# A recurrent attention kernel: working tiles allocated in the prepass, three buffers for the last tokens' V, seven late weight units, and other places for two stores in the loop

## The chip, the cores and the metric

The kernel runs on one core of one Trainium2 chip. The metric is the device time of one execution in microseconds (us). The time before is the median of three runs, 1682.81 us (1679.15 to 1693.0).

The core has five engines with a queue of instructions each: PE (matrix products), ACT and DVE (copies and elementwise work), POOL (a few elementwise operations and transfers), and SP, which only issues transfers. Engines wait for each other by semaphores. In the profile PE's weight loads have a row of their own, PEld.

## The reference

Two attention branches over the same 2048 tokens of 640 features, mixed by a gate. Branch A is recurrent: 64 segments of 32 tokens, each with 8 memory tokens ahead of it; the memory of a segment is the output of the segment before.

```python
for s in range(n_seg):                       # 64, seg_len 32, M = 8 memory tokens
    xs = x[:, s * seg_len:(s + 1) * seg_len, :]
    h = jnp.concatenate([mem, xs], axis=1)   # 40 tokens
    q, k, v = (jnp.einsum('btd,dhe->bhte', h, W) for W in (Wq, Wk, Wv))   # 32 heads of 192
    scores = jnp.einsum('bhqe,bhke->bhqk', q, k) * scale
    p = _softmax(jnp.where(mask, scores, -1e9), axis=-1)
    o = jnp.einsum('bhte,hed->btd', jnp.einsum('bhqk,bhke->bhqe', p, v), Wo)
    mem = o[:, :M, :]
    outs.append(o[:, M:, :])
...
g = sigmoid((x * gate_w).sum(-1))
return g * A(x) + (1 - g) * B(x)             # B: dilated local attention, not recurrent
```

## The kernel before

The program runs in four stretches.

**Part B** (`part_b`) computes branch B for all tokens, leaves the result and the gate in `bsc_dram`, and writes the tokens of all segments, transposed, to `xh_dram`. Behind it the first weights of branch A are loaded.

**The prepass** (`prepass`) projects the last 8 tokens of each of the 64 segments ahead of the loop, since they don't depend on the memory. First Q and K, by tiles `ZS` of two buffers that ACT's queue stores to `zpk_dram`; then V: three column groups `t` by four token groups `st`, 20 matmuls each (L548) into four PSUM banks, copied by ACT and DVE in turn (`evac`, L73 and L75) into a tile `ZV` of two buffers, and stored to `zpk_dram` by four transfers on ACT's queue (L555). PSUM holds eight banks, so two such steps. Before the V steps `load_late(1)` (L429) loads 24 weight units into the space that Q and K have left; it issues on SP.

**Part A** (`part_a`) is the recurrence. Its working tiles are allocated at its start: `PP` (aP: queries and values of a segment), `KW` (aK: keys, probabilities, output), `vz` (aVz), `sel` (aSel: selectors and masks that `build_sel` makes with DVE memsets and POOL's affine selects, reading ones from aP), `h_` (aH: the 40 tokens, transposed) and `a4` (aG). Weights don't all fit: 21 half units, listed in `STREAM`, are loaded again in each segment through seven slots (`wst`). `pump` issues such a load on SP as soon as the slot is free, that is when PE has used the unit that was there (`release`); `held` stops the issue, `stage` lets it go on. All engines' orders are written out by hand (`manual_schedule`).

A segment has two parts. The **head** projects the queries and keys of the first two thirds: `m_qk(i, kcs)` are the matmuls (L714; i even for queries, odd for keys), `c_qk(i)` ACT's copy out of PSUM (L721) and `t_qk(i)` DVE's transposition (L731, L734). The copy of i = 2 goes by way of `KW[:, 512:1024]`, all others by aP. The head also finishes the segment before: `pick` copies the new memory into aH, `tail` and `mix` (L664) blend the output, and `store_z` (L648, on POOL) writes the outputs of the 8 tokens from two places, `zst = [KW[:, 640:832], vz[:, 0:192]]`, to `oz_dram`. The **rest** does i = 4 and 5, the values (`m_v`, L811, `c_v`, L819), scores, softmax, the products with the values (`pv_half`, copied out by `c_o`, L853, and `c_z`, L859) and the output projection (`o_group`, L874: columns "oa" and "ob").

The loop (L1017) runs over segments 1 to 62: rest of one, head of the next, 62 passes. It resets its semaphores in a staggered way: the body has four stages (`tc.stage_boundary`), and no engine enters a stage before all engines have said that their work of the stage but one before is done. `done(engine)` in the code is where an engine waits for its own work of the previous stage, its transfers too, and says so. In the head the stage begins with `stage()`, followed by the stores and `done(POOL)`; `done(SP)` and `done(PE)` stand at its end.

**Part Z** (`part_z`) multiplies the outputs of the 512 tokens of the prepass with the output weights and writes them.

Of the kernel before, what the change touches and what calls it, by code (L numbers as in the profile page):

```python
# [10 lines left out]
BF = mybir.dt.bfloat16  # L11
# [2 lines left out]

SLOTS = 7
N_EARLY = 9
LATE0 = 101376
STREAM = [("q", 0, 1, 1), ("k", 0, 1, 1), ("k", 0, 3, 1), ("q", 1, 1, 0), ("k", 1, 0, 0), ("k", 1, 3, 1), ("q", 2, 2,
          0), ("k", 2, 0, 1), ("k", 2, 1, 1), ("k", 2, 4, 1), ("v", 0, 3, 1), ("v", 1, 1, 0), ("v", 1, 4, 1), ("v", 2,
# [7 lines left out]
class _K:  # L27
# [381 lines left out]
    def weights_setup(self):  # L409
        nc, tc = self.nc, self.tc  # L410
        rest = [k for u in self.slice_keys() for k in self.parts(u) if k not in STREAM]
        first = ["q", "k", "v", "oa", "ob"]
        rest = sorted(rest, key=lambda k: first.index(k[0]))
        self.early, late = rest[:N_EARLY], rest[N_EARLY:]
        self.late = ([], [], late[-3:])
        used = 0
        for k in late[:-3]:
# [85 lines left out]
    def prepass(self):  # L503

        nc, tc, KC = self.nc, self.tc, self.KC
# [3 lines left out]
        with tc.tile_pool(name="pre_zv", bufs=2, side="right", reuse_waits="tile") as zvp:  # L509
            zTi = zvp.tile([128, KC, NZ], BF, name="zTi", bufs=1)  # L510
            with tc.tile_pool(name="pre_zs", bufs=2, reuse_waits="tile") as zp, \
                    tc.tile_pool(name="pre_zt", bufs=1, reuse_waits="tile") as ztp:
                zT = ztp.tile([128, KC, NZ], BF, name="zT")
                nc.scalar.dma_start(zT[:], self.zT_dram[:].rearrange("p c s i -> p c (s i)"))
                nc.gpsimd.tensor_copy(zTi[:].rearrange("p c (i s) -> p c i s", i=8),
                                      zT[:].rearrange("p c (s i) -> p c i s", i=8))
                for m in ("q", "k"):
                    n = 16 if m == "q" else 24
                    for c in range(48):
                        if c % n == 0:  # L520
                            ZS = zp.tile([128, nseg, 192], BF, name="ZS")
                        if c % 16 == 0:
                            sls = [self.get_columns(m, c // 16, kc) for kc in range(KC)]
                        ps = self.pst([128, NZ], F32, name="ps_pre")
                        for kc in range(KC):
                            nc.tensor.matmul(ps[:], lhsT=sls[kc][c % 16],
                                             rhs=zT[:, kc, :], start=(kc == 0), stop=(kc == KC - 1))
                        zc = 8 * (c % 16) if m == "q" else 16 * (c % 12) + 8 * (c // 12 % 2)
                        self.evac(ZS[:, :, zc:zc + 8], ps[:].rearrange("p (s i) -> p s i", i=8))
                        if c % n == n - 1:  # L530
                            if m == "q":
                                zs = [(256 * (c // n) + 128, 0, 128)]
                            elif c < n:
                                zs = [(0, 0, 128), (256, 128, 64)]
                            else:
                                zs = [(320, 0, 64), (512, 64, 128)]
                            for z0, f, w in zs:
                                nc.scalar.dma_start(self.zpk_dram[:, :, z0:z0 + w].rearrange("s p f -> p s f"),
                                                    ZS[:, :, f:f + w])
            self.load_late(1)  # L540
            for t in range(3):
                sls = [self.v_columns(t, kc) for kc in range(KC)]
                for st in range(NZ // 128):
                    ZV = zvp.tile([128, 2048], BF, name="ZV")
# [8 lines left out]
                    for k in range(2 * st, 2 * st + 2):  # L553
                        for e, R, x, n in self.V_PIECES[t]:
                            nc.scalar.dma_start(self.zpk_dram[:, 8 * R + k:128:32, 768 + x:768 + x + n],  # L555
                                                ZV[64 * (k % 2):64 * (k % 2) + 64, :].rearrange(
                                                    "s (j e) -> s j e", j=4)[:, :, e:e + n])

    def build_sel(self, W, ones):
        nc = self.nc  # L560
# [26 lines left out]
    def part_a(self):  # L587
# [2 lines left out]
        scale_a = float(self.Dh) ** (-0.5)  # L590
        ctx = ExitStack()
        with ctx:
            pers = ctx.enter_context(tc.tile_pool(name="a_pers", bufs=1))
            work = ctx.enter_context(tc.tile_pool(name="a_work", bufs=1))
            PP, KW, vz, sel, h_, a4 = (pers.tile([128, n], BF, name=x) for x, n in (
                ("aP", 2304), ("aK", 1024), ("aVz", 384), ("aSel", 188), ("aH", 160), ("aG", 162)))
            self.build_sel(sel, PP[:, 0:160])
# [36 lines left out]
            def row(t, s):  # L634
                return t[bass.ds(s, 1)].rearrange("o p f -> p (o f)")

            def load_seg(s, dst=xh):
                nc.sync.dma_start(dst, row(self.xh_dram, s))

            def load_z(s):  # L640
                nc.sync.dma_start(PP[:, 0:2304].rearrange("p (g f) -> p g f", g=3)[:, :, 0:256],
# [7 lines left out]

            def load_a4(s):  # L650
                nc.sync.dma_start(a4[:].bitcast(I32), self.bsc_dram[bass.ds(32 * s, 32)].rearrange("t j f -> j t f"))

            load_seg(0, h_[:])
            load_z(0)
            load_vz(0)

            def tail():
                pa = Ss[0][:, 0, :]
# [22 lines left out]
            def segment(part, prev, s, nxt, looped=False):  # L681
# [217 lines left out]
                if part == "head":  # L899
                    self.used = 0  # L900
                    m_qk(0, (0, 1, 2))
                    stage()
                    if prev is not None:
                        store_z(prev, 0)
                        store_z(prev, 1)
                    done(POOL)
                    m_qk(1, (0,))
                    if prev is not None:
                        pick("ob", Ss[1])
# [3 lines left out]
                        burst(ms)  # L913
                    m_qk(0, (3, 4)); m_qk(1, (3, 4))
                    if prev is not None:
                        mix(pa)
                    done(DVE)
                    c_qk(0); c_qk(1)
                    done(ACTE)
                    t_qk(0); t_qk(1)  # L920
                    m_qk(2, range(KC)); c_qk(2); t_qk(2)
                    m_qk(3, range(KC)); c_qk(3); t_qk(3)
                    done(SP)
                    done(PE)
                    return
                self.end = len(STREAM) if nxt is None else None
# [50 lines left out]
                for i2 in range(4):  # L977
                    o_group("oa", i2)
                stage()
                if nxt is None:  # L980
                    store_z(s, 0)
                done(POOL)
                pairs = pv_half(1)
                done(PE)
                c_o(1, pairs)
                c_z(1, pairs, 0); c_z(1, pairs, 1)
                done(ACTE)
                if nxt is None:
                    store_z(s, 1)
                if nxt is None:  # L990
                    self.sort_oz(0)
                for i2 in (4, 5):
# [17 lines left out]

            ctx.enter_context(tc.manual_schedule(engines=set(ALL)))
            self.start_stream()
            segment("head", None, 0, 1)
            segment("rest", None, 0, 1)
            self.sent -= len(STREAM)
            segment("head", 0, 1, 2)
# [68 lines left out]
def kernel(  # L1085
# [20 lines left out]
    with tc.tile_pool(name="psum", bufs=8, space=bass.MemoryType.PSUM) as k.psum:  # L1106
        with tc.issue_after(k.first_store):
            k.prepass()
    k.load_late(2)
    k.part_a()  # L1110

_INS = ['A_x', 'A_mem0', 'A_Wq', 'A_Wk', 'A_Wv', 'A_Wo', 'A_seg_len', 'B_x', 'B_wqkv', 'B_wo', 'gate_w']
# [29 lines left out]
```

## Time and profile before

| what | value |
|---|---|
| profiled execution, its own time | 1679.99 us |
| its span, first to last instruction | 1678.5 us |
| mean granted TensorE clock | 0.981 |
| PE busy | 1486.7 us, 89% of the span |
| DVE, ACT, POOL busy | 802.7, 656.1, 143.2 us |
| transfers | 438.32 MB, mean 261 GB/s |
| streamed weight loads (`wst<-wscr`) | 965 of 256 KB and 384 of 192 KB |
| loop | from about 461 to 1594 us |

The span and the profiled time differ by 1.5 us, which lie outside the program's instructions. Idle time of an engine is given with the one that ended it ("<-"). A matmul's end is modelled in the profile, so a PE that waits a little for a streamed weight can still look busy.

### The profile page before, as it was taken

How to read it: one execution, taken by the hardware profiler on the slowest of the kernel's cores; microseconds unless marked ns; L12 is line 12 of the kernel's file. 1: busy time of each engine (PE TensorE's matmuls, PEld its weight loads, DVE VectorE, ACT ScalarE, POOL GpSimd, SP SyncE). 2: the span in 40 equal slices, each digit the busy share in tenths (PEclk: the TensorE clock that was granted, in tenths of full speed). 3: DMA queues.
4: the chain of work that ended last, by engine and by line, in shares of the span. 5: the costliest groups of instructions: out<-in, count | busy, mean ns of one | idle time of the engine just before them, and what ended most of it. 6: DMA issues, size and time to landing. Idle time of an engine off the chain costs nothing. (4 is left out here: it accounts for less than half of the span.)

```text
span 1678.5 us, 91617 instructions
## 1 busy us (share of the span) xinstructions
PE 1486.7 (89%) x37462; PEld 852.0 (51%) x37477; DVE 802.7 (48%) x1936; ACT 656.1 (39%) x1609; POOL 143.2 (9%) x275
## 2 busy tenths in 40 slices
PE   6898897997689999999999999999999999999878
PEld 3455553343345555555555555555555555555457
DVE  4556542222345555555555555555555555555520
ACT  3766741212233433433433433443443343443340
POOL 4002000000200010010000001001001001001000
PEclk9999999999799999999999999999999999999989
DMA  6931059789679999999999999999999999999981
GB/s 165 215 101 53 31 157 266 181 204 290 213 247 317 307 316 318 301 305 320 307 300 318 314 301 311 314 306 317 315 303 312 316 305 310 317 310 310 316 209 28
DMA packets 438730, 438.32 MB, mean 261 GB/s; under 512 B 194172, under 2 KB 306820, under 8 KB 438660
## 3 DMA queue, kind: packets, MB, share of 16 engines
q1 hardware_dynamic: 344344, 395.02, 73.2%
q10 hardware_dynamic: 87148, 29.72, 7.2%
q0 software_dynamic: 7168, 12.60, 2.2%
q8 instruction: 51, 0.84, 0.2%
q14 instruction: 19, 0.16, 0.0%
HBM read 402.83 MB, written 39.48 MB: 264 GB/s over the span
## 5 line engine op out<-in xcount | busy, mean ns | idle before, releaser
L714 PEld LDWEIGHTS <-aH 128*32 128x32 bf16 x7680 | 201.2, 96 | 277.2 <-PE psm L714 79.6
L811 PE MATMUL psm<-wlate_v,aH 128*32 128x512 bf16 x3200 | 250.9, 382 | 18.1 <-DVE aP L819 16.7
L721 ACT CAST aP<-psx 128x512 bf16<-128x512 f32 x128 | 68.8, 589 | 327.9 <-PE psx L714 327.9
L714 PE MATMUL psx<-wlate_k,aH 128*32 128x512 bf16 x1920 | 195.6, 385 | 0.0
L874 PEld LDWEIGHTS <-aP 128*32 128x32 bf16 x6144 | 160.1, 96 | 64.1 <-ACT aP L853 23.1
L874 PE MATMUL psm<-wlate_oa,aP 128*32 128x384 bf16 x2560 | 167.7, 329 | 0.0
L714 PE MATMUL psm<-wlate_q,aH 128*32 128x512 bf16 x1408 | 108.8, 381 | 59.7 <-ACT aK L721 50.6
L734 DVE STREAM_TRANSPOSE aK<-aP 128x512 bf16<-128x512 bf16 (+1 forms) x256 | 142.6, 557 | 13.4 <-ACT aP L721 0.3
L714 PE MATMUL psx<-wst,aH 128*32 128x512 bf16 x768 | 138.8, 384 | 3.4 <-DMA wst<-wscr 3.4
L811 PEld LDWEIGHTS <-aH 128*32 128x32 bf16 x3840 | 94.5, 97 | 82.5 <-issue 20.0
L731 DVE STREAM_TRANSPOSE aP<-aP 128x512 bf16<-128x512 bf16 x128 | 91.1, 712 | 89.2 <-ACT aP L721 89.0
L874 PE MATMUL psm<-wst,aP 128*32 128x384 bf16 (+1 forms) x896 | 128.9, 306 | 4.7 <-DMA wst<-wscr 4.7
L874 PE MATMUL psm<-wlate_ob,aP 128*32 128x256 bf16 x2688 | 125.3, 273 | 0.4 <-issue 0.4
L811 PE MATMUL psm<-wst,aH 128*32 128x512 bf16 x640 | 124.7, 383 | 0.0
L714 PE MATMUL psx<-wres_q,aH 128*32 128x512 bf16 x1152 | 97.4, 385 | 19.1 <-DMA aH<-xh_dram 14.6
L853 DVE CAST aP<-psx 128x128 bf16<-128x128 f32 (+2 forms) x192 | 75.6, 422 | 70.5 <-PE psx L841 70.4
L773 ACT ACTIVATE aK<-psS 128x224 bf16<-128x224 f32 x128 | 46.1, 360 | 148.8 <-PE psS L765 148.8
L774 DVE TENSOR_TENSOR aK<-aK,aSel 128x224 bf16<-128x224 bf16 x128 | 35.3, 275 | 139.1 <-ACT aK L773 138.6
L714 PE MATMUL psm<-wst,aH 128*32 128x512 bf16 x512 | 99.6, 380 | 0.9 <-DMA wst<-wscr 0.6
L853 ACT CAST aP<-psS 128x384 bf16<-128x384 f32 (+2 forms) x192 | 65.4, 375 | 83.5 <-PE psx L841 81.6
L648 POOL DMA_DIRECT2D oz_dram<-aK x64 | 34.6, 541 | 734.8 <-DMA aVz<-zpk_dram 712.9
L819 ACT CAST aP<-psm 128x512 bf16<-128x512 f32 x128 | 75.4, 589 | 47.3 <-PE psS L765 45.0
(164 smaller groups left out, 2750.5 us busy)
## 6 DMA issues: line engine op xcount, KB each, us to landing
wst<-wscr SPq DMA_DIRECT2D x965, 256.0 KB, 4.4
wst<-wscr SPq DMA_DIRECT2D x384, 192.0 KB, 3.5
aP<-zpk_dram SPq DMA_DIRECT2D x64, 192.0 KB, 3.1
zpk_dram<-ZS ACTq DMA_DIRECT2D x5, 2048.0 KB
aVz<-zpk_dram POOLq DMA_DIRECT2D x64, 96.0 KB, 4.0
wlate_k<-in_A_Wk_dram SPq DMA_DIRECT2D x8, 512.0 KB
wres_q<-in_A_Wq_dram SPq DMA_DIRECT2D x7, 512.0 KB
wst<-in_A_Wk_dram SPq DMA_DIRECT2D x14, 256.0 KB
```

The source lines that it names most:

```text
L648: nc.gpsimd.dma_start(row(self.oz_dram[h], s), zst[h])
L714: burst([nc.tensor.matmul(pq[32 * j:32 * j + 32, :], lhsT=hT[:, kc, :], rhs=sl[j], start=(kc == 0), stop=(kc == KC - 1), tile_position=(0, ...
L721: nc.scalar.copy(st[i], pqs[i])
L731: nc.vector.transpose(P[p][:, 1:5, :, :].rearrange("p b c i -> p c b i"), st[i])
L734: nc.vector.transpose(KT[:, c0:c1, :].rearrange("p c k -> p (c k)"), st[i] if part is None else st5[part])
L773: nc.scalar.activation(E, pSs[h][:, :, 0:112], ACT.Exp, scale=scale_a)
L774: nc.vector.tensor_tensor(out=E, in0=E, in1=self.mask[h].unsqueeze(1).to_broadcast([128, 2, 112]), op=ALU.mult)
L811: burst([nc.tensor.matmul(pvs[t][32 * j:32 * j + 32, :], lhsT=hT[:, kc, :], rhs=sl[j], start=(kc == 0), stop=(kc == KC - 1), tile_position ...
L819: (nc.vector.tensor_copy if t == 0 else nc.scalar.copy)(Px[t], pvs[t][:])
L853: (nc.scalar.copy, nc.vector.tensor_copy)[g](x.rearrange("p (j c q) -> p j c q", j=2, q=32), pairs[g][:, :, 0:240].rearrange("p j (c q) -> ...
L874: ms.append(nc.tensor.matmul(pso[part][32 * jj:32 * jj + 32, 0:n], lhsT=oT_slot(R // 2, j, 3 * (R % 2) + t), rhs=self.o_weights(osl, part, ...
```

## The change

1. In the prepass, ahead of the V steps, a new function `working_tiles` allocates the six working tiles of part A and calls `build_sel`; their pool waits tile by tile for the space it takes over. aH's first load is issued there too, behind `load_late(1)`, no longer at the start of part A. The first loads of aP and aVz now follow `start_stream`.
2. `ZV` has three buffers instead of two.
3. `N_LAST`: the last seven weight units (ob 1, half of 2, 3, 4, 5, half of 6, 7) instead of the last three (ob 5, half of 6, 7) are loaded by `load_late(2)`, and that stands behind the first head, not ahead of part A. `load_late(1)` has 20 units instead of 24.
4. In the loop the first `store_z` moves from the head of the next segment to the rest, right behind the boundary in the output projection, and the second behind the copies that it reads. A DVE memset of one column of `zst[0]` stands ahead of `mix`. `done(POOL)` comes with the head's boundary; `done(ACTE)` moves behind `c_qk(2)`, and `done(SP)` with it, ahead of the second key group.

```diff
+N_LAST = 7
...
-        self.late = ([], [], late[-3:])
+        self.late = ([], [], late[-N_LAST:])
...
+            self.working_tiles()
             self.load_late(1)
+            nc.sync.dma_start(self.work[4][:], self.xh_dram[0:1].rearrange('o p f -> p (o f)'))
...
-                    ZV = zvp.tile([128, 2048], BF, name="ZV")
+                    ZV = zvp.tile([128, 2048], BF, name="ZV", bufs=3)
...
+    def working_tiles(self):
+
+        pers = self.ctx.enter_context(self.tc.tile_pool(name="a_pers", bufs=1, reuse_waits="tile"))
+        PP, KW, vz, sel, h_, a4 = self.work = [pers.tile([128, n], BF, name=x) for x, n in (
+            ("aP", 2304), ("aK", 1024), ("aVz", 384), ("aSel", 188), ("aH", 160), ("aG", 162))]
+        self.build_sel(sel, PP[:, 0:160])
...
-            load_seg(0, h_[:])
-            load_z(0)
-            load_vz(0)
...
                     m_qk(0, (0, 1, 2))
-                    stage()
-                    if prev is not None:
-                        store_z(prev, 0)
-                        store_z(prev, 1)
-                    done(POOL)
+                    stage(POOL)
...
                     if prev is not None:
+                        nc.vector.memset(zst[0][:, 0:1], 0.0)
                         mix(pa)
                     done(DVE)
                     c_qk(0); c_qk(1)
-                    done(ACTE)
                     t_qk(0); t_qk(1)
-                    m_qk(2, range(KC)); c_qk(2); t_qk(2)
+                    m_qk(2, range(KC)); c_qk(2)
+                    done(ACTE, SP)
+                    t_qk(2)
                     m_qk(3, range(KC)); c_qk(3); t_qk(3)
-                    done(SP)
                     done(PE)
...
                 stage()
-                if nxt is None:
-                    store_z(s, 0)
+                store_z(s, 0)
                 done(POOL)
...
-                if nxt is None:
-                    store_z(s, 1)
+                store_z(s, 1)
...
             self.start_stream()
+            load_z(0)
+            load_vz(0)
             segment("head", None, 0, 1)
+            self.load_late(2)
...
-    k.load_late(2)
     k.part_a()
```

More of the change, by code (lines that the diff above doesn't have):

```diff
@@ L414, in weights_setup @@
         self.early, late = rest[:N_EARLY], rest[N_EARLY:]
-        self.late = ([], [], late[-3:])
+        self.late = ([], [], late[-N_LAST:])
         used = 0
-        for k in late[:-3]:
+        for k in late[:-N_LAST]:
             used += 2 * self.width(k)
@@ L592, in part_a @@
         with ctx:
[L593 to L597, printed above, removed]
+            PP, KW, vz, sel, h_, a4 = self.work
             p0 = (128, 896, 1664)
@@ L635, in row, with load_seg @@
                 return t[bass.ds(s, 1)].rearrange("o p f -> p (o f)")
-            def load_seg(s, dst=xh):
-                nc.sync.dma_start(dst, row(self.xh_dram, s))
+            def load_seg(s):
+                nc.sync.dma_start(xh, row(self.xh_dram, s))
             def load_z(s):
```

## The prediction

> **What bounds the kernel.** I read the page first (TensorE is busy 89% of the span and the transfers 90% or more in most slices), then the groups of instructions for what ended PE's idle time, the timeline of some passes of the loop, the windows for the transfers' share, and the timeline between the third projection of the last tokens (L548) and the first pass.
>
> Groups, columns: busy us, mean ns | idle before, and who ended it.
>
> ```profile
> L721 ACT CAST aK<-psm 128x512 bf16<-128x512 f32 x64 | 37.5, 586 | 70.4 <-DMA oz_dram<-aK 45.6 <-PE psm L714 24.9
> L714 PE MATMUL psm<-wlate_q,aH 128*32 128x512 bf16 x1408 | 108.8, 381 | 59.7 <-ACT aK L721 50.6 <-ACT aP L721 2.5 <-PEq L1017 2.4
> L548 PE MATMUL ps_pre<-wlate_v,zTi 128*128 128x512 bf16 x195 | 49.2, 385 | 7.2 <-DVE ZV L75 6.7 <-issue 0.2
> ```
>
> The largest removable idle time of PE in the loop is 50.6 us ahead of `m_qk(4)`: it waits for ACT's copy of the third projection into `aK`, and that copy waits for a store of `aK`. One pass:
>
> ```profile
> 1025.96 0.54 POOL L648 DMA_DIRECT2D oz_dram<-aK  x1 [11.41 <-DMA aVz<-zpk_dram]
> ...
> 1030.93 0.59 ACT L721 CAST aK<-psm 128x512 bf16<-128x512 f32 x1 [1.72 <-DMA oz_dram<-aK]
> ...
> 1031.57 0.62 PE L714 MATMUL psm<-wlate_q,aH 128*32 128x512 bf16 x8 [0.94 <-ACT aK L721]
> ```
>
> The store is issued at 1025.96, lands 4.87 us later (1030.83 by its semaphore), and the copy starts 0.10 us after that. In the 40 passes I compared, the copy starts at most 0.2 us after this landing, also where the profile names PE. Over 59 passes PE's pause there is 0.82 to 1.75 us, mean 0.89, of a mean pass of 18.12 us (shortest 17.90).
>
> But the same pause has a second cause behind it. SP's `done(SP)` is the last thing SP does in the head; its signal comes at 1030.98, PE's first step into the next pass at 1031.04, and PE needs another 0.53 us to its first matmul. Both causes end within 0.1 us of each other. And there is a third bound, the transfers:
>
> ```profile
> 1002.00:1004.00 2.00, 1.83 (x62) 0.83 (x61) 1.24 (x5) 1.60 (x5) 0.00 (x0) 1.00 0.83 258
> 1004.00:1006.00 2.00, 2.00 (x86) 1.59 (x78) 0.83 (x3) 0.68 (x3) 0.00 (x0) 1.00 0.79 231
> ...
> 1010.00:1012.00 2.00, 2.00 (x42) 1.56 (x33) 1.20 (x2) 1.07 (x2) 0.00 (x0) 1.00 1.04 402
> 1012.00:1014.00 2.00, 1.13 (x25) 0.55 (x24) 1.13 (x3) 1.07 (x2) 0.00 (x0) 1.00 1.06 396
> ```
>
> The last two columns are the transfers' share and GB/s: 0.79 to 0.83 while the output projection starts, full (396 to 402 GB/s) in the head and just where PE pauses (1.13 busy of 2). Matching landings with first use, the streamed units of the head land a mean 0.3 us before use; 97 of 354 such uses come within 0.1 us of the landing. PE runs there at the transfers' pace, and the pause is in part time in which they catch up.
>
> Before the loop:
>
> ```profile
> 413.31 2.10 PE L548 MATMUL ps_pre<-wlate_v,zTi 128*128 128x512 bf16 x9
> 430.05 1.04 PE L714 MATMUL psx<-wres_q,aH 128*32 128x512 bf16 x6 [14.64 <-DMA aH<-xh_dram]
> ...
> 440.63 0.61 PE L714 MATMUL psx<-wst,aH 128*32 128x512 bf16 x2 [3.40 <-DMA wst<-wscr]
> ```
>
> ```profile
> 420.06 1.07 ACT L73 CAST ZV<-ps_pre 128x512 bf16<-128x512 f32 x2 [5.20 <-DMA zpk_dram<-ZV]
> ```
>
> ```profile
> 427.98 0.19 DVE L561 MEMSET aP<- 128x160 bf16 x1 [9.46 <-DMA zpk_dram<-ZV]
> ```
>
> ```profile
> SPq L641 <- POOL aSel L584: 8.4, 1, 8.4
> ```
>
> ```profile
> 410.00:420.00 10.00, 5.36 (x25) 2.25 (x23) 2.58 (x4) 2.15 (x4) 0.00 (x0) 0.96 0.88 230
> 420.00:430.00 10.00, 0.00 (x0) 0.00 (x0) 0.59 (x7) 1.07 (x2) 1.30 (x5) 0.50 0.70 189
> 430.00:440.00 10.00, 7.18 (x102) 3.27 (x103) 2.73 (x4) 2.25 (x4) 6.47 (x33) 0.84 0.24 69
> 440.00:450.00 10.00, 9.13 (x242) 4.61 (x245) 3.96 (x11) 3.76 (x11) 0.00 (x0) 0.67 0.84 275
> ```
>
> PE stands 14.64 us, until the first tokens (`aH`) are in; their tile lies in space that the last V stores free. Then SP waits 8.4 us for the selector that POOL builds before it may load `aP`, and the weights behind that load come 3.40 us late. A measurement of this kernel tells about 1% (17 us) from no change.
>
> **The change, part by part.** Times are against the profiled execution (span 1678.5, 1.5 around it, 1680.0), 2.8 under the median of 1682.8.
>
> (1) V phase. It lasts from 353.6 to 415.4, 61.8 us, for 240 matmuls that follow each other at 0.216 us: 51.8 us. The other 10 are waits, mostly for a ZV buffer (the ACT line above, and the group's 6.7). A third buffer lets each copy wait for a store one step (4.3 us) older, and four units (10,752 bytes x 128 partitions = 1.38 MB, at the 350 GB/s of this stretch 3.9 us) leave the queue. Against it stands DVE's memset of `aP`, now beside the V copies: it waits for the last store of ZS, issued at 354.5 and landed at 367; V copies queued behind it on DVE (the first two are at 357.7 and 362.0) would be up to 9 us late, and PE, with two steps of PSUM, some 5. Bounds: 10 us gained, 5 lost; I take **-4**, as three buffers and fewer loads act in nearly all of the twelve steps and the memset once.
>
> (2) The pause. `aH` and the selector are ready in the V phase. Left is what frees PSUM: two copies each on ACT (1.07) and DVE (1.29) and a hand-over, 2 us. 14.6 - 2 = **-12.6**; -8 if the last copy still waits 5 us for a store.
>
> (3) After it. SP no longer waits for the selector, so the 3.40 us go. The granted clock in the two windows behind the pause is 0.84 and 0.67, which costs 7.18 x 0.16 + 9.13 x 0.33 = 4.2 us; I take half, since (4) brings a pause of its own. **-5.4**, between -3.4 and -7.6. The Trainium skill ("TensorE: Matmul & The Clock Gate", Part 1) says that one idle window of some 3.4 us halves the clock until a busy window has passed; by that a pause costs 1.7 us, and with two pauses this term would again be -6.8, the whole sum 1.4 lower. The clock rows agree in kind (0.50 in the pause).
>
> The first loads of `aP` and `aVz` now stand behind the seven first slots on SP and behind the last V store on POOL; they are wanted at `scores(0)` and `pv_half(0)`, some 7 and 12 us after the head starts, so I cost them at nothing (late, they would hold those steps by up to the 3 us that such a load takes).
>
> (4) Seven units instead of three: 18,432 x 128 = 2.36 MB, issued by SP behind the head's six refills and only when the last V store has landed; 6.7 us at 350 GB/s. Queued behind them on SP are the refills for `v(2,0)` and all after it, needed some 12 us after the head starts. Cost 0 to 7; I take **+5**, since the transfers have little slack left there: their idle share in 400 to 470 adds up to 20 us, and (1) to (3) use 22.
>
> Before the loop: -4 - 12.6 - 5.4 + 5 = **-17**, bounds -7 and -24.
>
> (5) The loop. Both stores move up: the first from 16.6 us after the pass's mix (L664) to about 12.6, the second from 17.3 to 14. They land 3.5 to 5.3 us after issue, so by 17 to 19, while the copy wants `aK` at 19 to 20: that wait goes. The wait is now DVE's (the memset of one column, 60 ns by L565, in the 0.4 us that DVE waits for PE ahead of L664; uncovered it is 62 x 0.06 = 4 us). SP's `done` comes before the refills for the second key group, so PE goes on after its own branch: 1030.49 + 0.53 = 1031.02 instead of 1031.57. ACT's `done` also moves, behind the copy; only the next copy (`c_qk(3)`) stands behind it, which waits for PE: nothing. PE alone would gain **0.55** a pass.
>
> The transfers don't give that. From the first streamed load after the output stage's boundary (12.6) to the landing of the load that `m_qk(5)` needs (23.1) the queue never empties: a mean 10.44 us over 59 passes. The rest of the pass, from that load's use back to 12.6, takes 7.5 us where nothing waits. 10.44 + 7.5 = 17.94, or 0.18 a pass less than now. One of the two stores (0.12 us of all 16 engines) may move into the stretch with share 0.8, so 0.30. Bounds 0 and 0.55; I take 0.30, as the landings are the nearer row: 62 x 0.30 = **-18.6**. `load_vz` also comes 0.9 us earlier and lands among the same loads; their later slack is 0.7 or more.
>
> Sum: 1680.0 - 17 - 18.6 = 1644.4; with 2.8 to the median **1647**.
>
> **Rivals.** A: the transfers pace the loop wholly. For it: the just-in-time landings. Against: the slack of 0.2 at the last of them. Loop 0, start -7 to -17: 1666 to 1676. B: the transfers follow PE, as PE's releases come earlier and a share of 0.8 leaves room in the output stage: loop -34, start -17 or more: 1632 or less. C, the other side: SP, in order, now waits for all loads of its last stage (`done(SP)`) before it issues two refills. They go out up to one transfer (0.66 us) later; where fewer than 2.2 us of loads stand ahead (issue to first packet), the queue runs dry each pass: 62 x 0.66 = +41, less 17: 1707. Now five loads (3.3 us) stand ahead, which speaks against it. D: the early tiles don't help, because the V copies stand behind the memset and the late units behind the V stores: start -2, loop as forecast: 1662.
>
> **How the numbers follow.** Forecast (1632 to 1660) 0.50; A 0.17; B 0.14; C 0.09; D 0.10. Faster by over 1% (under 1666) takes the forecast, B and D: 0.74; A within 1%: 0.17; C slower: 0.09. The range 1622 to 1676 leaves out C and the far end of B.
>
> **What would show it.** Right: no `oz_dram<-aK` behind ACT L721; PE's pause ahead of `m_qk(4)` under 0.4 us; a mean pass of 17.8; PE's pause before the first projections 2 to 4 us. Wrong: passes still at 18.1 with PE waiting for `wst` instead (A); passes near 17.5 (B); SP's issues bunched late in the head (C); DVE idle before the V copies until 367 (D).

## The result, and the profile after

The changed kernel takes 1663.08 us, median of four runs (1660.96 to 1666.07); the kernel before took 1685.95 beside it (four runs, 1679.15 to 1693.0). The ratio is 0.9856, 95% interval 0.9825 to 0.9887: 1.4% faster. The profiled executions have spans of 1659.5 and 1678.5 us, 19.0 apart.

The groups of instructions after (busy us, mean ns | idle before, and who ended it):

```profile
L723 ACT CAST aK<-psm 128x512 bf16<-128x512 f32 x64 | 37.5, 586 | 10.7 <-PE psm L716 4.4 <-DVE aP L733 3.6
L716 PE MATMUL psm<-wlate_q,aH 128*32 128x512 bf16 x1408 | 112.7, 382 | 14.6 <-PE psm L716 6.5 <-issue 2.5 <-PEq L1017 1.6
L791 PE MATMUL psS<-aK,aSel 128*32 128x160 bf16 (+1 forms) x1024 | 36.1, 216 | 21.3 <-DVE aK L736 13.4 <-issue 1.2
```

The copy of the third projection (now L723) no longer waits for `oz_dram<-aK`, and PE's idle time in its group (now L716) is 14.6 us instead of 59.7. A new line has come up: 21.3 us ahead of the sums of the exponentials (`e_sum`, L791), where 2.9 us stood before; 13.4 of it are put down to DVE's transposition of the last keys. One pass, whose mix is at 1033.6 (the next at 1051.3):

```profile
1045.95 0.54 POOL L654 DMA_DIRECT2D oz_dram<-aK  x1 [8.41 <-ACT aK L861]
...
1053.43 0.59 ACT L723 CAST aK<-psm 128x512 bf16<-128x512 f32 x1 [0.21 <-PE psm L716]
...
1054.78 0.62 PE L716 MATMUL psm<-wlate_q,aH 128*32 128x512 bf16 x8 [0.33 <-PE psm L716]
```

PE's pause ahead of `m_qk(4)` is 0.33 us here, a mean 0.175 over 59 passes (0.887 before). The mean pass is 17.92 us (18.12 before), the shortest 17.13 (17.89 before). The transfers in another pass (last columns: granted clock, transfers' share, GB/s), first while the head's units are loaded, then around the start of the output projection:

```profile
1000.00:1002.00 2.00, 1.80 (x43) 1.07 (x47) 0.84 (x2) 0.45 (x1) 0.54 (x1) 1.00 0.99 355
1002.00:1004.00 2.00, 2.00 (x84) 1.12 (x76) 0.76 (x2) 1.11 (x3) 0.00 (x0) 1.00 0.99 333
...
1008.00:1010.00 2.00, 1.85 (x84) 1.19 (x84) 0.86 (x5) 1.31 (x6) 0.50 (x1) 1.00 0.80 220
1010.00:1012.00 2.00, 2.00 (x64) 1.62 (x56) 0.98 (x4) 0.47 (x3) 0.58 (x2) 1.00 0.77 229
```

The shape is that of before: full in the head, 0.77 to 0.80 at the output projection. Ahead of the loop, from the timeline:

```profile
410.78 1.03 PE L551 MATMUL ps_pre<-wlate_v,zTi 128*128 128x512 bf16 x4
411.28 5.65 ACTq L558 DMA_DIRECT2D zpk_dram<-ZV  x4
416.98 0.59 ACT L74 CAST ZV<-ps_pre 128x512 bf16<-128x512 f32 x1 [5.19 <-DMA zpk_dram<-ZV]
417.62 1.01 PE L716 MATMUL psx<-wres_q,aH 128*32 128x512 bf16 x5 [5.81 <-ACT ZV L74]
...
437.51 0.61 PE L813 MATMUL psm<-wst,aH 128*32 128x512 bf16 x2 [8.07 <-DMA wst<-wscr]
```

```profile
418.70 4.97 SPq L464 DMA_DIRECT2D wst<-wscr  x6
423.72 7.04 SPq L430 DMA_DIRECT2D wlate_ob<-in_A_Wo_dram  x7
430.86 4.99 SPq L464 DMA_DIRECT2D wst<-wscr  x7
```

```profile
420.00:430.00 10.00, 9.19 (x246) 4.96 (x239) 5.68 (x12) 5.06 (x12) 0.72 (x1) 0.97 1.01 306
430.00:440.00 10.00, 2.49 (x70) 1.14 (x73) 0.75 (x4) 0.62 (x2) 0.00 (x0) 0.71 1.08 311
```

The pause of 14.64 us has shrunk to 5.81. What ends it is ACT's last copy: ACT's queue first issues the four stores of the step before, and that row lasts 5.65 us. The four issues themselves take 2.53 of it (0.54 to 0.82 each), as in other steps. By the trace's semaphore events the second store waits 3.04 us ahead of its issue, for semaphore 100: a streamed weight load that SP issued at 410.91 has the same one and landed at 414.85, 0.02 us before the store went out. The same wait, of 2.1 to 3.4 us, stands ahead of the same store in the eight other profiles with this start, ACT's stores and all bytes (experiments 2, 3, 4, 7, 8, 9, 11 and 12). Then comes a new pause of 8.07 us: PE waits for the refill of `v(2,0)`, and SP can issue it only at 430.86, behind 7.04 us of the seven late units. The transfers are full all the while.

The 19.0 us, by points that can be read off the starts in both timelines (first matmul of the V phase; its last end; first matmul of the first scores; DVE's mixes of segments 0, 1 and 62):

| stretch | before | after | difference |
|---|---|---|---|
| up to the V phase (nothing changed there) | 353.6 | 351.4 | -2.2 |
| V phase | 61.8 | 60.4 | -1.4 |
| its end to the first scores | 26.3 | 13.3 | -13.0 |
| first scores to first mix | 15.2 | 21.8 | +6.6 |
| first to second mix (entry of the loop) | 25.6 | 29.0 | +3.4 |
| second to 63rd mix (61 passes) | 1106.0 | 1092.9 | -13.1 |
| rest | 90.0 | 90.7 | +0.7 |

So the start gives 6.6 us, of which 2.2 are no work of the change, and the loop 13.1. Both vary from one execution to the next: the same loop took 1096.8 to 1099.5 us in five other profiles of this study (experiments 1, 3, 4, 10 and 12), and the old loop 1109.8 in experiment 2. By the means (1107.9 of two, 1097.5 of six) the loop's edits are worth 10.5 us, 0.17 a pass.

### The profile page after: what moved, and what is told of

The parts are those of the page before. It is cut to its first block, busy times and chain, and to the rows that moved or that the text cites. A ratio compares the mean times of both kernels' runs of the same rounds, so it can differ in the third digit from the quotient of the medians.

```text
span 1659.5 us, 91540 instructions
## 1 busy us (share of the span) xinstructions
PE 1505.6 (91%) x37462; PEld 858.0 (52%) x37477; DVE 804.2 (48%) x1999; ACT 666.3 (40%) x1609; POOL 143.6 (9%) x275
## 5 line engine op out<-in xcount | busy, mean ns | idle before, releaser
L716 PEld LDWEIGHTS <-aH 128*32 128x32 bf16 x7680 | 208.6, 96 | 226.0 <-issue 41.5
L813 PE MATMUL psm<-wlate_v,aH 128*32 128x512 bf16 x3200 | 254.8, 380 | 4.5 <-DVE aP L821 3.5
L723 ACT CAST aP<-psx 128x512 bf16<-128x512 f32 x128 | 68.7, 589 | 330.2 <-PE psx L716 326.4
L716 PE MATMUL psx<-wlate_k,aH 128*32 128x512 bf16 x1920 | 198.7, 383 | 0.0
L716 PE MATMUL psx<-wst,aH 128*32 128x512 bf16 x768 | 138.4, 383 | 2.3 <-DMA wst<-wscr 1.9
L813 PEld LDWEIGHTS <-aH 128*32 128x32 bf16 x3840 | 93.6, 97 | 77.1 <-issue 14.1
L716 PE MATMUL psm<-wlate_q,aH 128*32 128x512 bf16 x1408 | 112.7, 382 | 14.6 <-PE psm L716 6.5
L716 PE MATMUL psx<-wres_q,aH 128*32 128x512 bf16 x1152 | 103.1, 388 | 10.1 <-ACT ZV L74 5.8
L716 PE MATMUL psm<-wst,aH 128*32 128x512 bf16 x512 | 100.0, 381 | 2.3 <-SPq L1017 1.6
L716 PE MATMUL psm<-wlate_k,aH 128*32 128x512 bf16 x1024 | 86.5, 379 | 0.0
```

The lines of the kernel that those rows point to most:

```text
L716: burst([nc.tensor.matmul(pq[32 * j:32 * j + 32, :], lhsT=hT[:, kc, :], rhs=sl[j], start=(kc == 0), stop=(kc == KC - 1), tile_position=(0, ...
L723: nc.scalar.copy(st[i], pqs[i])
L813: burst([nc.tensor.matmul(pvs[t][32 * j:32 * j + 32, :], lhsT=hT[:, kc, :], rhs=sl[j], start=(kc == 0), stop=(kc == KC - 1), tile_position ...
```

## The experiments

Each ran beside the kernel before; differences in time are between the medians of the same set. The stretches of the table above come from each run's own timeline.

### The loop alone, the start alone, two buffers, a later place

**1.** The loop's edits in the kernel before:

```diff
-                    stage()
-                    if prev is not None:
-                        store_z(prev, 0)
-                        store_z(prev, 1)
-                    done(POOL)
+                    stage(POOL)
...
+                        nc.vector.memset(zst[0][:, 0:1], 0.0)
...
-                    done(ACTE)
...
+                    done(ACTE, SP)
...
-                    done(SP)
...
-                if nxt is None:
-                    store_z(s, 0)
+                store_z(s, 0)
...
-                if nxt is None:
-                    store_z(s, 1)
+                store_z(s, 1)
```

> The kernel before with only the loop's edits (both stores one stage sooner, SP's and ACT's done behind the third projection's copy). Theory (the passes are now paced by the transfers that end with the load for m_qk(5), and the start's edits have no part in it): mean pass 17.9 us against 18.1, PE's pause ahead of m_qk(4) under 0.4 us, time 12 to 13 us below the kernel before (62 x 0.20). By the prediction's term 18.6 us below. Rival (the loop's gain in the changed kernel comes from the early tiles or the seven late units, which shift the state in which the loop is entered): pass stays at 18.0 to 18.1, time within 5 us of the kernel before.

1669.06 against 1685.41, -16.4 (ratio 0.9903, 0.9874 to 0.9932). The 61 passes take 1099.5 us, 6.5 less than in the profile of before and 10.3 less than in the next experiment, which has the old loop. PE's pause has gone as in the changed kernel:

```profile
L714 PE MATMUL psm<-wlate_q,aH 128*32 128x512 bf16 x1408 | 112.8, 382 | 13.3 <-PE psm L714 4.9 <-DVE aK L734 2.4 <-PEq L1012 1.8
```

The time is 3 us further down than expected, while the mean pass, 18.02, stays short of the 17.9: the passes hold 6.5 to 10.3 of the 16.4 us, and the profile, of the slowest of the four runs, does not show the rest. That PE's pause goes, and the passes get shorter, needs nothing of the start.

**2.** The changed kernel with the old loop (the same diff, backwards):

> The changed kernel with the loop of the kernel before. Theory (the start gives 16.6 us up to the first scores and loses 10 of them to the seven late units, in the first segment and at the loop's entry): first scores at 425, first mix at 447 and second mix at 476 against 442, 457 and 482 before; pass 18.1; time 6 to 7 us below the kernel before. By the prediction's sum 17 us below. Rival (the start's loss belongs to the loop's new places of stores and done, through the first pass): second mix at 472 or earlier, time 10 us or more below.

1678.20 against 1685.41, -7.2 (0.9956, 0.9938 to 0.9974), as the theory had it. First scores 14.3 us behind the V phase's end, 22.2 from there to the first mix, 25.8 to the second. The start loses its gain in the first segment without the loop's edits. All these points came 2 to 6 us later than expected, as the V phase began at 354.9.

**3.** Two ZV buffers:

```diff
-                    ZV = zvp.tile([128, 2048], BF, name="ZV", bufs=3)
+                    ZV = zvp.tile([128, 2048], BF, name="ZV")
```

> The changed kernel with two ZV buffers again. Theory (the V phase is paced by the transfers and by ACT's issuing of the stores, not by the number of buffers): last V matmul within 2 us of 411.5, time within 2 us of the changed kernel. By the prediction's term (1) two buffers cost up to 4 us.

1670.64 (1660.59 to 1675.33) against 1685.41 (0.9910, 0.9872 to 0.9947): by times alone not told from the changed kernel. The V phase takes 60.8 us; with three buffers and ACT's stores it took 58.1 to 61.1 in nine profiles of this study, mean 59.4. The third buffer is worth some 1.4 us, within that spread.

**4.** The late units behind the refills of the next stage:

```diff
             segment("head", None, 0, 1)
-            self.load_late(2)
             segment("rest", None, 0, 1)
...
                 stage(POOL)
+                if prev is None:
+                    self.load_late(2)
                 e_sum(0)
```

> The changed kernel with the seven late units issued later, behind the refills of the second value stage's boundary instead of right behind the first head. Theory (PE's 8.1 us wait in the first segment is the refill for v(2,0) standing on SP behind 7.0 us of late loads): that wait falls under 2 us, a shorter wait of up to 4 us comes at the output projection for the late units, first mix at 441 to 444 instead of 446.9, time 3 to 6 us below the changed kernel. Rival (all of the first segment's transfers pace it, in whatever order): first mix at 446 to 448, the wait only moves to the output projection, time the same within 2 us.

1666.40 against 1685.41 (0.9881, 0.9849 to 0.9912). The wait for `v(2,0)` is gone, as the theory said, but first scores to first mix take 21.0 us instead of 21.8: PE waits 4.26 us for a refill at the output projection instead, and 2.11 us ahead of the products with the values; what ended the latter the profile doesn't tell.

```profile
439.22 0.19 PE L837 MATMUL psS<-aK,aP 32*128 32x40 bf16 x2 [2.11 <-issue]
...
446.25 0.51 PE L876 MATMUL psm<-wst,aP 128*32 128x384 bf16 x2 [4.26 <-DMA wst<-wscr]
```

The rival is right here: the order on SP's list is worth 1 us, the wait moves.

### What the seven late units cost

**12.** No loads for the seven units:

```diff
         for k in ks:
-            self.load(k, tiles[k][:])
+            if part == 2:
+                self.nc.gpsimd.memset(tiles[k][:], 0.0)
+                self.res_tiles[k] = self.view(tiles[k][:], k)
+            else:
+                self.load(k, tiles[k][:])
```

> The changed kernel without the loads of the seven late units: POOL fills their tiles with zeros instead, at the same place in the program, so 2.36 MB less are moved in the first segment and SP has no late units to issue. Theory (the bytes of the seven units, not their place on SP's list, take back 6 to 10 us of the start's gain): the stretch from the first scores to the first mix falls from 21.8 us to 15 to 17 (15.2 in the kernel before), PE's wait of 8.1 us ahead of v(2,0) under 1.5 us, the second mix 6 to 10 us sooner after the V phase's start, passes of the loop unchanged at 17.9 to 18.0, time 6 to 10 us below the changed kernel. Rival (segment 0 is held by its 21 refills and SP's other work, late units or not): stretch of 19 us or more, time within 3 us.

1653.44 against 1677.37 (0.9850, 0.9821 to 0.9878): -23.9, where the changed kernel had -22.9 beside its own set; the times don't show the difference that was expected, and that it reaches the end is not shown. The profile shows a gain in the first segment. First scores to first mix take 13.0 us, 8.8 less than in the changed kernel and 2.2 less than before the change. PE has no pause over 0.7 us there:

```profile
418.00:428.00 10.00, 9.69 (x308) 5.54 (x304) 6.21 (x14) 5.46 (x14) 6.45 (x6) 1.00 0.98 338
428.00:438.00 10.00, 9.16 (x256) 5.42 (x248) 4.52 (x15) 3.51 (x11) 3.31 (x5) 1.00 0.91 300
```

The granted clock stays at 1.00, where it was 0.71 in the window of the 8.07 us pause. The Trainium skill ("TensorE: Matmul & The Clock Gate", Part 1) has an idle window of some 3.4 us halve the clock; the clock rows with and without the pause agree with it. A pause of that length isn't needed, though: in the changed kernel the clock is 0.51 from 454.60 to 458.10 too, behind a stretch of 3.40 us in which PE was still busy for 0.83 us. From the V phase's start to the second mix it is 113.0 us against 124.5 (119.9 to 123.4 in experiments 2, 3, 7, 8, 9 and 11, which keep the seven loads in their place). Its 61 passes took 1098.0 us, which is the usual time of this loop; the changed kernel's profile, with 1092.9, is the quick one.

### One cause or two

**7.** SP's `done` back at the end of the head:

```diff
-                    done(ACTE, SP)
+                    done(ACTE)
                     t_qk(2)
                     m_qk(3, range(KC)); c_qk(3); t_qk(3)
+                    done(SP)
```

> The changed kernel with SP's done back at the end of the head; the stores and ACT's done stay where the change put them. Theory (two causes of the pause end within 0.1 us of each other, so one alone gains nothing): no oz_dram<-aK behind the copy of the third projection, but PE's pause ahead of m_qk(4) is still 0.8 to 0.9 us, pass 18.1, time 10 to 13 us above the changed kernel. Rival (the store alone made the pause): pause under 0.4 us, pass 17.9, time as the changed kernel.

**8.** The stores back in the next head, no memset, `done(ACTE, SP)` as changed:

```diff
-                    stage(POOL)
+                    stage()
+                    if prev is not None:
+                        store_z(prev, 0)
+                        store_z(prev, 1)
+                    done(POOL)
...
-                        nc.vector.memset(zst[0][:, 0:1], 0.0)
...
-                store_z(s, 0)
+                if nxt is None:
+                    store_z(s, 0)
...
-                store_z(s, 1)
+                if nxt is None:
+                    store_z(s, 1)
```

> The changed kernel with the two stores back behind the first projections of the next pass, and without the memset; SP's and ACT's done stay where the change put them. Theory (as before): the copy of the third projection waits for oz_dram<-aK again, PE's pause ahead of m_qk(4) is 0.8 to 0.9 us, pass 18.1, time 10 to 13 us above the changed kernel. Rival (SP's done alone made the pause): pause under 0.4 us, pass 17.9, time as the changed kernel.

Against 1682.11: 1672.79 (0.9950, 0.9927 to 0.9974) and 1666.73 (0.9904, 0.9867 to 0.9940). The second, 15.4 us down, lies between the start alone (-7.2) and the changed kernel (-22.9), and by its time alone it wouldn't decide; what follows rests on one profile of each. The 61 passes take 1111.6 and 1105.3 us, no better than before (1106.0). The groups of 7, then of 8:

```profile
L716 PE MATMUL psm<-wlate_q,aH 128*32 128x512 bf16 x1408 | 111.9, 383 | 56.0 <-DVE aP L733 27.7 <-ACT aP L723 23.6 <-issue 3.0
...
L723 ACT CAST aK<-psm 128x512 bf16<-128x512 f32 x64 | 37.4, 585 | 11.9 <-PE psm L716 7.1 <-DVE aP L733 2.1
```

```profile
L716 PE MATMUL psm<-wlate_q,aH 128*32 128x512 bf16 x1408 | 108.7, 380 | 59.1 <-ACT aK L723 54.6 <-DVE aK L736 2.4 <-PEq L1022 2.1
...
L723 ACT CAST aK<-psm 128x512 bf16<-128x512 f32 x64 | 37.5, 586 | 81.6 <-DMA oz_dram<-aK 64.8 <-PE psm L716 16.8
```

In 7 the copy waits for no store and PE still stands 56.0 us; the profile names DVE and ACT there, though only SP's `done` differs from the changed kernel: a releaser in such a line may just be what ended last among things long due. In 8 the copy waits for the store again. With one cause left the pause stays, at a mean of 0.84 and 0.87 us a pass, and the mean pass doesn't gain; it does with both gone. The two are not quite equal: the shortest pass of 7 is 17.89 us, as before the change, that of 8 is 17.48, so with the store alone left the floor is lower, and the mean pass of 8 doesn't reach it.

### What paces the pass now

**5 and 6.** Half the bytes for the streamed units of q and k, in the changed kernel and in the kernel before:

```diff
-            self.nc.sync.dma_start(self.slots[n][:, 0:self.width(k)], self.wscr[k])
+            w = self.width(k) // (2 if k[0] in 'qk' else 1)
+            self.nc.sync.dma_start(self.slots[n][:, 0:w], self.wscr[k][:, 0:w])
```

> The changed kernel, where the streamed units of q and k load only the first half of their bytes in each pass (their other columns keep stale values); the numbers of loads, waits and matmuls stay. It takes 1.3 MB of 4.7 MB off the stream of a pass. Theory (the transfers pace the loop; PE alone would gain 0.55 a pass or more): mean pass 17.1 to 17.3 us, near the shortest pass of the changed kernel (17.13), PE's pauses at the sums of the exponentials (L791) gone, time 38 to 50 us below the changed kernel. Rival (the passes are paced by the hand-overs between PE, ACT and DVE behind m_qk(5), not by bytes): pass 17.8 to 17.9, time within 8 us of the changed kernel.

> The same halving in the kernel before. Theory (there the store's landing and SP's done hold the pass at a floor of its own, whatever the transfers do): pass 17.9, its shortest so far, PE's pause ahead of m_qk(4) still 0.8 us, time 8 to 15 us below the kernel before, and 0.6 to 0.8 us a pass above the halved changed kernel. Rival (the pause only let the transfers catch up; with less to carry it shrinks): pass under 17.5.

5: 1608.72 against 1682.11 (0.9577, 0.9540 to 0.9614), 73.4 below the kernel before and so some 50 below the changed one. 6: 1665.25 (0.9898, 0.9855 to 0.9941), 16.9 below, 2 us more than expected. The groups, 5 and then 6:

```profile
L717 PE MATMUL psm<-wlate_q,aH 128*32 128x512 bf16 x1408 | 106.8, 384 | 8.4 <-DVE aK L737 2.4 <-PEq L1018 1.6
...
L792 PE MATMUL psS<-aK,aSel 128*32 128x160 bf16 (+1 forms) x1024 | 35.6, 215 | 2.7 <-DVE aK L737 0.7
```

```profile
L715 PE MATMUL psm<-wlate_q,aH 128*32 128x512 bf16 x1408 | 106.4, 382 | 56.0 <-DVE aP L732 51.8 <-DVE aK L735 2.5 <-PEq L1018 1.7
```

The passes of 5 are 17.14 us with hardly any spread (17.13 to 17.25), those of 6 are 17.91 (17.90 to 17.95, but for the first, 18.30). This is the floor of each program with the transfers out of the way: the old places hold every pass at 17.9, and the edits are worth 0.77 us a pass. The changed kernel, with all bytes, gets 0.20 of it. The rest goes with the bytes of the transfers: the windows of the same 1000 us of the loop, the changed kernel first, then 5:

```profile
500.00:1500.00 1000.00, 947.68 (x28360) 546.60 (x28352) 537.76 (x1454) 414.55 (x1118) 90.75 (x167) 1.00 0.94 314
```

```profile
500.00:1500.00 1000.00, 961.78 (x29660) 539.83 (x29652) 560.34 (x1518) 427.81 (x1166) 95.65 (x176) 1.00 0.81 252
```

0.94 x 17.92 is 16.8 us a pass of the 16 transfer engines' time, against 17.13 that PE needs. By this sum alone a pass of 17.13 would fit, but the share was only 0.77 to 0.80 around the start of the output projection. How much of the rest is the total of bytes, and how much their place in the pass, is not separated here: halving takes bytes from the whole pass.

**9.** The output projection's stage boundary ahead of its first groups:

```diff
+                stage()
+                store_z(s, 0)
+                done(POOL)
                 for i2 in range(4):
                     o_group("oa", i2)
-                stage()
-                store_z(s, 0)
-                done(POOL)
```

> The changed kernel with the output projection's stage boundary (and the first store and POOL's done with it) ahead of its first four groups instead of behind them. Between SP's hold in front of that boundary and the boundary itself the transfers' share is 0.79 to 0.84 in the changed kernel, and the first refill behind it goes out 12.4 us after the mix, 1.2 us after the one ahead of the hold. Theory (the chain of transfers that starts with this refill paces the pass): the refill goes out 0.5 to 0.9 us sooner against the mix, mean pass 17.4 to 17.7 us, time 12 to 30 us below the changed kernel. Rival 1 (the transfers are at their total limit, not at this chain's start): pass 17.9, time the same within 5 us. Rival 2 (the boundary is uncovered there, PE waits for the engines' hand-over ahead of the output projection): pass 18.2 or more, time 15 us or more above the changed kernel.

1698.77 against 1684.40 (1.0082, 1.0059 to 1.0106): slower, rival 2. The refill goes out at 12.5 us, no sooner: SP's list has nothing between the hold and the boundary, so moving the boundary against PE's matmuls moves nothing on SP. And PE now stands in every pass, 0.77 us:

```profile
L876 PE MATMUL psm<-wlate_oa,aP 128*32 128x384 bf16 x2560 | 168.3, 330 | 47.7 <-ACT aP L821 43.6 <-ACT psS L800 3.0 <-ACT aK L861 1.0
```

What it waits for there in truth was not settled.

**11.** What held the refill was SP's own order: behind the mix the loads for the next segment are issued at 9.41, then two more, then a refill at 11.26, then SP's 0.6 us of boundary steps, then the refill at 12.43, 1.24 us after the matmuls that free its slot. So two of the loads go elsewhere:

```diff
...
-                    load_z(nxt)
-                    load_a4(s)
+                    load_z(nxt, nc.gpsimd)
+                    load_a4(s, nc.scalar)
```

> The changed kernel with two of the three loads for the next segment taken off SP's list, at the same place in the program: the last tokens' rows (aP) issued by POOL, the mix's rows (aG) by ACT. In the changed kernel SP needs 0.56 to 0.6 us for each of the three (9.38, 9.94, 10.54 after the mix) and 0.6 for its own steps over the stage boundary, so the refill that starts the chain goes out at 12.40, 1.2 us after the end of the matmuls that release its slot (11.18). Theory (SP's order of issue, not the total of bytes, sets the start of the chain that paces the pass): this refill goes out at 11.2 to 11.5, the transfers' share between 11 and 14 us of the pass rises over 0.9, mean pass 17.3 to 17.6, time 18 to 37 us below the changed kernel. Rival 1 (the total of bytes at the rate of the transfers sets the pass): refill earlier, but the landings of the chain and the pass of 17.9 stay, time within 5 us. Rival 2 (ACT's 0.58 us of issue or POOL's later second store hold PE): pass 18.0 or more, with a new PE wait behind ACT or at the store.

1653.85 against 1684.07 (0.9827, 0.9792 to 0.9862), -30.2. It is the fastest version with all of the work, though its interval overlaps the changed kernel's. The refill now follows its matmuls by 0.18 us. The 61 passes take 1085.7 us; the same loop without this edit took 1092.9 in the changed kernel and 1098.5, 1099.0 and 1098.0 in experiments 3, 4 and 12. That is 7 to 13 us, less than the 18 that the theory wanted, and this profile is of the quickest of its six runs. The mixes also come less evenly, 16.13 to 19.91 us apart. SP's list in one pass, and the loop's windows:

```profile
1000.93 0.34 SPq L644 DMA_DIRECT2D aK<-xh_dram  x1
1001.37 16.49 SPq L464 DMA_DIRECT2D wst<-wscr  x21
```

```profile
500.00:1500.00 1000.00, 946.28 (x28596) 529.26 (x28588) 539.29 (x1464) 416.51 (x1126) 136.49 (x225) 1.00 0.95 316
```

0.95 x 17.79 is 16.9 us of transfers a pass, as before: the chain starts sooner, but the same bytes take the same time. Theory and rival 1 share the result: by this profile SP's order cost 0.1 to 0.2 us a pass. What is left above 17.14 went when bytes were halved (experiment 5).

### The stores of the V phase

**10.** POOL issues them:

```diff
-                            nc.scalar.dma_start(self.zpk_dram[:, 8 * R + k:128:32, ...
+                            nc.gpsimd.dma_start(self.zpk_dram[:, 8 * R + k:128:32, ...
```

> The changed kernel with the V phase's stores issued by POOL instead of ACT. Theory (the last pause of 5.8 us ahead of the first projections is ACT, whose four stores of the step before take 5.65 us to issue, in order, ahead of its last copy): the pause falls to 2 to 3 us and the V phase itself gets 2 to 5 us shorter; as the first segment is paced by its transfers, only 0 to 4 us of it reach the end: time 0 to 6 us below the changed kernel. Rival (the transfers hold the copies through the ZV buffers, and POOL issues these stores of many short rows more slowly): V phase the same or longer, pause still 5 us or more, time the same or above.

1745.91 against 1684.40 (1.0357, 1.0328 to 1.0387): the rival, and far worse than it said. On POOL the stores follow each other by some 2.7 us; on ACT four take 2.55 us where none of them waits:

```profile
436.36 0.58 POOL L558 DMA_DIRECT2D zpk_dram<-ZV  x1 [2.10 <-issue]
439.05 0.58 POOL L558 DMA_DIRECT2D zpk_dram<-ZV  x1 [2.10 <-issue]
```

```profile
407.01 2.55 ACTq L558 DMA_DIRECT2D zpk_dram<-ZV  x4
```

Four of them make 10.7 us a step, against 4.3 of matmuls, and the V phase takes 106.3 us. The Trainium skill ("DMA: Bandwidth & Descriptors", Issuing engine by pattern) calls transfers from SP and ACT generally faster than those of POOL; for these stores the trace agrees, by a factor of four in the issue. The theory had also misread the 5.65 us: more than half of it was the second store's wait for a weight load, not ACT's time to issue.

## Why the prediction was right or wrong

It said 1647 us, faster by over 1% with 0.74, and a range of 1622 to 1676. The time is in the range and the sign is right, but 16 us above the number: of a forecast gain of 35.6 us in the profiled execution 19.0 came. The stretch that the forecast gave itself, 1632 to 1660, is missed by 3 us; the time lies between it and rival A's (1666 to 1676), and the range holds it because it takes in A.

The larger miss is the start. It was forecast at -17, bounds -7 and -24; from the V phase's start to the second mix 4.4 us came in this pair, and 6.4 by the means (128.3 in the two profiles with the old start and all bytes, 121.9 in the seven with the new one, its late units in their place and ACT's stores). These bounds were tighter than those of the terms, which add up to +0.6 and -30.2.

**(1) V phase, -4:** measured -1.4 in this pair, -2.5 by the means (61.9 in the three profiles with the old start, 59.4). The term was too large, above all the credit for the third buffer: each copy may wait for an older store, but experiment 3 lost only some 1.4 us without it. That the full transfers and ACT's own order of issue make the copies late is what the lines suggest; it was not taken apart. Waits of a store for a weight load's semaphore occur here too: one issued at 393.94 waited 2.30 us for a load of `wlate_oa`.

**(2) The pause, -12.6:** measured -8.8 (14.64 to 5.81). The prediction named this outcome as its weaker bound (-8, if the last copy still waits 5 us for a store) and chose the other. The copy does stand 5.19 us, behind four stores that ACT issues first, and 3.04 of that is the second store's wait for the weight load. The profile of before had shown 5.20 us ahead of a copy of the last step, and nothing in the change touched ACT's order.

**(3) After it, -5.4:** first projections to first scores took 11.64 and take 7.45 us, -4.2, within its bounds (the term's own sum, 3.4 and half of 4.2, is 5.5). SP no longer waits for the selector.

**(4) Seven late units, +5, bounds 0 and 7:** mis-sized. First scores to first mix is 6.6 us longer, still within the bounds, but experiment 12's profile puts the units' cost at 8.8 us in this stretch alone, over the upper one; its time does not confirm that. The prediction let slack in the transfers swallow part of 6.7 us. But the changed start brings the first segment's refills into that same slack: the windows from 420 to 440 are full. With it comes a pause long enough to lower the clock. The entry of the loop was 3.4 us longer in this pair; over the other profiles with the new start that stretch varies from 24.0 to 27.9, so no cause is claimed for it.

**(5) The loop, 0.30 a pass:** measured 0.20 in this pair and 0.17 by the means. The arithmetic of the chain was right: 10.44 us from the first refill behind the boundary to the landing that `m_qk(5)` needs, plus 7.5, gave 0.18. The chain now measures 10.39. The 0.12 added for a store that would leave it was wrong: the store is issued 0.3 us behind that refill and stays among the same loads. The bound for PE alone (0.55) was too low: 0.77 by experiments 5 and 6. The prediction kept 0.53 us for PE's own branch into the next pass; PE's pause falls to 0.07 us with the transfers out of the way, so that branch lies beside the matmuls that are still running.

**What would show it:** no store behind the copy, yes; pause under 0.4 us, yes; mean pass 17.8, nearly (17.92); pause before the first projections 2 to 4 us, no (5.81).

**Rivals.** A and B bracket the loop: A said that PE would wait for `wst` instead. The new wait at L791 bears it out in part, for it falls from 21.3 to 2.7 us with half the bytes (experiment 5); but 13 us of gain remain. C did not come: the refill behind SP's `done` went out 0.36 us later in the head (2.14 to 2.50 us after the mix), and in the pass shown above the transfers' share stays at 0.99 to 1.00 there. D did not come as told: DVE stood 2.7 us for the memset of `aP`, at 365.7, with copies of V ahead of it and behind it. The start fell short for the reasons under (1), (2) and (4).

A reading that misled: PE's idle time per pass fell by 0.55 us (1.49 to 0.94), the pass by only 0.20. PE's busy time rose from 16.63 to 16.97 us a pass with the same instructions, and is 16.48 in experiment 5. Short waits seem to be counted in the matmuls there: the busy time goes back when half the bytes are left out.

## What to carry to other kernels

When two causes of a wait end together, remove both, and then ask what the wait was covering: here the transfers needed 16.8 us of a 17.9 us pass, and only a quarter of the gain that PE alone would have had came. Halving the bytes of the loads, in both kernels, measures each program's own floor in one run. Ahead of a loop, price moved loads by the bytes that already stand in the new place, not by the idle share that the old timeline showed; and read an in-order queue from its own list, since a boundary or a load moved in the program moves a refill only if it stands ahead of it on that engine. A long row of issues in a timeline can hold a wait: take its single issues and semaphores before calling it the cost of issuing.

## What the runs showed of the hardware that was not expected

- PE's step over a stage boundary costs nothing visible when it isn't held: 0.07 us of pause in experiment 5 against 0.85 in 6.
- Four stores took ACT 2.55 us to issue; the four ahead of the last copy took 5.65 us, 3.04 of them a wait for a weight load of SP with the same semaphore. ACT's copies stand behind them in order. The same stores cost POOL some 2.7 us each.
- SP needs 0.55 to 0.7 us for each of the three small loads of a pass, from one issue to the next, and 0.6 us for about ten semaphore steps of 0.06 us at a stage boundary, and in the changed kernel this list kept a refill back until 1.24 us after its slot was free.
- With the old floor gone the passes spread: 17.13 to 20.15 us after, 17.89 to 18.93 before.
